# One decode kernel, several edits at once: projection per group, last V load in pieces, V three steps behind K, denominator ahead of the values, K ahead of wq, wq over 128 partitions, wo early in longer rows

## Chip, cores, metric

One core of one Trainium2 chip runs the kernel. The metric is the device time in microseconds (us), median of several executions. Lower is better.

## The reference, cut to what matters

A decode step: one query token, 16 query heads in 8 groups of 2, a cache of 65,536 keys and values per group, head size 256, model width 448. A small mixer runs beside it and is mixed in by a gate.

```python
# cut: setup, mixer, gate
q = (x @ wq).reshape(B, Sq, Hq, Dh)                    # wq: 448 x 4096
scores = einsum("bhqd,bhkd->bhqk", q, k) * Dh ** -0.5  # k, v: 8 groups x 65536 x 256, bf16
p = softmax(scores, axis=-1)
o = einsum("bhqk,bhkd->bhqd", p, v)
a = o.reshape(B, Sq, Hq * Dh) @ wo                     # wo: 4096 x 448
return g * a + (1 - g) * b                             # b: the mixer's row
```

K and V are 537 MB together; with wq and wo 544 MB must come in, once.

## The kernel before

A *chunk* is 2048 keys, a *load* is two chunks of K or of V (2.1 MB). There are 256 chunks, so 128 K loads and 128 V loads, in two K buffers and three V buffers. The SP engine issues loads in pairs, K(n) and V(n-1). A K issue waits until the transposes of the load that held its buffer are done. In each step, PE (TensorE, the matmul engine) transposes chunk s (32 matmuls), computes the scores of chunk s-1 (32), and the values and the denominator of chunk s-2 (32 and 1); this distance of two steps is the *V lag*. VectorE and ScalarE copy the transposed K out of PSUM, the memory that matmuls write to, and ScalarE takes the exponential.

```python
            eng.dma_start(wq_sb, A_wq.rearrange("(kt c) n -> c kt n", c=KCP)).then_inc(sem_wq, 16)

            def k_dma(cd):
                c0 = cd * DC
                g, k = divmod(c0, NCPH)
                slot = cd % KB
                if cd >= KB:
                    eng.wait_ge(sem_tr, NB * ((cd - KB) * DC + DC))
                src = A_k_cache[0, g, k * CH:(k + DC) * CH, :].rearrange("(p n) d -> p (n d)", p=P)
            # ... cut ...
            WO_AT = max(0, NCD - 20)
            for cd in range(NCD + 1):
                if cd < NCD:
                    k_dma(cd)
                if cd - 1 >= 0:
                    v_dma(cd - 1)
                if cd == WO_AT:
                    eng.wait_ge(s_pe_pro, 3)
                    eng.dma_start(wo_sb, A_wo.rearrange("(kt p) n -> p kt n", p=P)).then_inc(sem_wo, 16)

            eng.wait_ge(sem_tail_v, 1)
            eng.dma_start(out_row_ap, out_b[:, :]).then_inc(sem_out, 16)
            eng.wait_ge(sem_out, 16)
            # ... cut ...
            for s in range(NC + 2):
                c = s
                if c < NC:
                    cdk, ck = divmod(c, DC)
                    slot = cdk % KB
                    if ck == 0:
            # ... cut ...
                        for dh in range(2):
                            j = 2 * ntl + dh
                            ins = pe.matmul(sps[:, sbk, 2 * nt:2 * nt + 2],
                                            ktT[:, slotT, bnk, j * P:(j + 1) * P],
                                            qT[:, dh, REP * g:REP * g + REP],
                                            start=(dh == 0), stop=(dh == 1))
                    ins.then_inc(sem_qk, 1)
                cp = c - 2
                if 0 <= cp < NC:
                    g, k = divmod(cp, NCPH)
                    pe.wait_ge(sem_exp, cp + 1)
                    cdv, cv = divmod(cp, DC)
                    vslot = cdv % VB
                    if cv == 0:
                        pe.wait_ge(sem_v[vslot], 16 * (cdv // VB + 1))
                    pslot = cp % PTB
                    for nt in range(NT):
                        for dh in range(2):
                            first = (k == 0 and nt == 0 and dh == 0)
                            last = (k == NCPH - 1 and nt == NT - 1 and dh == 1)
                            col = (g * 2 + dh) * REP
                            pe.matmul(po[:, col:col + REP],
                                      vbuf[:, vslot, cv, nt, dh * P:(dh + 1) * P],
                                      pT[:, pslot, 2 * nt:2 * nt + 2],
                                      start=first, stop=last)
                    ins = pe.matmul(den[0:1, g * 2 * NT:(g + 1) * 2 * NT], ones_col[:, 0:1],
                                    pT[:, pslot, 0:2 * NT], start=(k == 0), stop=(k == NCPH - 1))
                    ins.then_inc(sem_pv, 1)
            # ... cut ...
            pe.wait_ge(s_rden, 1)
            pe.matmul(den[:, RC:RC + HQ], ones_row_f[0:1, 0:P], rden[0:1, :], start=True, stop=True
                      ).then_inc(s_tp, 1)
            pe.wait_ge(s_oTn, 1)
            pe.wait_ge(sem_wo, 16)
            nmm = 2 * HQ
            i = 0
            for hq in range(HQ):
                g, hh = divmod(hq, REP)
                for dh in range(2):
                    col = g * 4 + dh * REP + hh
                    kt = 2 * hq + dh
                    i += 1
                    ins = pe.matmul(sps[0:1, 1, 0:DM], oTn[:, col:col + 1], wo_sb[:, kt, :],
                                    start=(i == 1), stop=(i == nmm))
            ins.then_inc(s_tp, 1)
```

Profile lines name source lines: in the kernel before L277 is the transposes, L293 the scores, L312 the values, L316 the denominator, L339 the projection, L188 and L197 the K and V issues.

The softmax here doesn't subtract the row's maximum and nothing guards it: scores larger than these inputs give would overflow.

## Time and profile before

| | before |
|---|---|
| device time, 3 runs | 1346.64 us (1344.35 to 1348.2) |
| span of the profiled execution | 1353.2 us |
| bytes in | 548 MB |
| mean granted TensorE clock | 0.74 |

The device time is about 1.8 us above the span wherever both are known for one execution. So the profiled execution took about 1355 us. It was slower than any timed one.

The page of the kernel before. Rows are 40 slices of 33.8 us; the clock and DMA rows are in tenths; then the DMA queues (packets, MB, share of 16 engines) and three groups (count, busy us, mean ns, idle before).

```profile
span 1353.2 us, 53303 instructions
...
PEclk9677767768677778676787767766867767777777
DMA  9999999999999999999999999999999999999993
GB/s 302 425 423 411 417 419 425 409 422 412 420 416 416 420 405 423 418 420 407 414 399 402 409 404 414 416 382 402 420 422 419 409 423 398 421 417 416 414 417 160
...
q1 hardware_dynamic: 41454, 544.24, 97.3%
q8 instruction: 198, 3.24, 0.9%
...
L277 PE MATMUL kst<-ident,kbuf 128*128 128x128 bf16 x8192 | 726.0, 269 | 26.0 <-issue 13.7
...
L312 PE MATMUL po<-pT,vbuf 128*128 128x2 bf16 x8192 | 251.3, 164 | 92.2 <-DMA vbuf<-in_A_v_cache_dram 57.5
...
L339 PE MATMUL sps<-wqo,oTn 128*1 128x448 bf16 x32 | 8.1, 424 | 0.6 <-DVE oTn L460 0.6
...
```

The stream runs near 420 GB/s in all slices but the first (302) and the last (160). PE is busy 88% of the span at a clock that changes between full and half. The row q8 is the fetching of instructions: 198 transfers of 16 KB.

Three windows of the same execution; the last three columns are granted clock, DMA share and rate.

```profile
...
core 0: us, PE busy (x) PEld busy (x) DVE busy (x) ACT busy (x) POOL busy (x), PEclk, DMA share, GB/s
...
4.00:20.00 16.00, 1.94 (x46) 1.40 (x45) 6.04 (x26) 1.69 (x3) 0.00 (x0) 1.00 1.00 265
20.00:44.00 24.00, 20.74 (x439) 20.55 (x440) 11.04 (x24) 8.80 (x13) 0.00 (x0) 0.81 1.00 422
44.00:1295.00 1251.00, 1119.29 (x23624) 1091.67 (x23622) 373.97 (x613) 519.62 (x744) 0.00 (x0) 0.74 1.00 414
...
```

From 4 to 20 us the DMA engines are busy all the time, yet only 265 GB/s arrive. That is when wq loads. In the middle the average is 414 GB/s.

What PE waited for (us in total, times, longest us). "issue" is time in which the profile shows no wait.

```profile
...
PE po L312 <- DMA vbuf<-in_A_v_cache_dram: 57.5, 56, 2.5
...
PE po L312 <- issue: 31.4, 32, 2.4
...
PE sps L293 <- issue: 21.2, 28, 1.9
...
PE kst L277 <- issue: 13.7, 17, 1.9
PE kst L277 <- DMA kbuf<-in_A_k_cache_dram: 12.1, 7, 9.6
...
```

PE waits for V, seldom for K. The "issue" times of L312, L293 and L277 sum to 66 us. They lie in the midst of groups of 32 equal matmuls, and their place moves on by 8 matmuls every four steps (13, 21, 29 matmuls left at 102, 122 and 142 us). A step has 97 matmuls with a weight load each, 194 instructions, and some waits. If it has 196, four steps are three blocks of 256 instructions and 16 instructions, or 8 matmuls, more. So I take these for stalls at block borders of the instruction stream; the block size is inferred from this shift.

The end of the timeline (start us, us, engine, line, what):

```profile
...
1339.59 0.19 PE L316 MATMUL den<-pT,ones_col 128*1 128x32 bf16 x1
1339.82 0.41 DVE L448 TENSOR_REDUCE densum<-den 1x16 f32<-1x256 f32 x1 [4.71 <-PE den L316]
...
1341.80 8.07 PE L339 MATMUL sps<-wqo,oTn 128*1 128x448 bf16 x32 [0.60 <-DVE oTn L460]
...
1349.91 0.61 DVE L467 CAST arow_b<-sps 1x448 bf16<-1x448 f32 x1 [7.24 <-PE sps L339]
...
1351.65 0.26 SPq L210 DMA_DIRECT2D out_dram<-out_b  x1
```

The last values end near 1339.7 us. The 32 projection matmuls after them take 8.1 us, and the span ends at 1353.2.

### The profile page before, as it was taken

The page shows a single profiled execution, that of the slowest core. Times are in us where ns is not written, and L with a number is a line of the kernel's source. Part 1 is how long each engine was busy: PE and PEld are TensorE (multiplying, and loading weights), DVE is VectorE, ACT ScalarE, POOL GpSimd, SP SyncE. Part 2 cuts the span into 40 slices and gives each one's busy share as a digit, 9 for nine tenths or more (in the row PEclk, how much of TensorE's full clock was granted, in tenths as well). Part 3 has the DMA queues.
Part 4 walks back from the last instruction along what each step waited for, and adds up shares of the span by engine and source line. Part 5 has one row for each costly group of instructions (what it writes and reads, how often), then busy time and mean ns, then how long its engine had stood idle before and what let it go on. Part 6 is the DMA issues. An engine that isn't in the chain of part 4 may idle for free.

```text
span 1353.2 us, 53303 instructions
## 1 busy us (share of the span) xinstructions
PE 1190.9 (88%) x25055; PEld 1156.5 (85%) x25055; DVE 405.9 (30%) x690; ACT 549.1 (41%) x786; POOL 1.2 (0%) x10
## 2 busy tenths in 40 slices
PE   4889898989989898989999888998899896888997
PEld 4889898889888898989888888888898896888886
DVE  3783222222222222222222222222222221222222
ACT  2454344434344344444434434433444442443442
POOL 0000000000000000000000000000000000000000
PEclk9677767768677778676787767766867767777777
DMA  9999999999999999999999999999999999999993
GB/s 302 425 423 411 417 419 425 409 422 412 420 416 416 420 405 423 418 420 407 414 399 402 409 404 414 416 382 402 420 422 419 409 423 398 421 417 416 414 417 160
DMA packets 41672, 547.65 MB, mean 405 GB/s; under 512 B 4136, under 2 KB 8235, under 8 KB 8238
## 3 DMA queue, kind: packets, MB, share of 16 engines
q1 hardware_dynamic: 41454, 544.24, 97.3%
q8 instruction: 198, 3.24, 0.9%
q14 instruction: 20, 0.16, 0.0%
HBM read 544.22 MB, written 0.00 MB: 402 GB/s over the span
## 4 chain that ended last, share of the span: by engine, by line
DMA 50%; PE 44%; issue 4%; SPq 1%; ACT 0%; DVE 0%; DVEq 0%; ACTq 0%
DMA vbuf<-in_A_v_cache_dram 50%; PE kst L277 28%; PE po L312 9%; PE sps L293 5%; PE den L316 1%; SPq L188 1%; PE sps L339 1%; PE po L322 0%; ACT ktT L497 0%; ACT pT L503 0%; SPq L197 0%; PE den L327 0%; DVE arow_b L467 0%; DVE densum L448 0%; DVE out_b L472 0%
## 5 line engine op out<-in xcount | busy, mean ns | idle before, releaser
L497 ACT ACTIVATE ktT<-kst 128x1024 bf16<-128x1024 bf16 x512 | 513.5, 1022 | 763.6 <-PE kst L277 763.6
L277 PE MATMUL kst<-ident,kbuf 128*128 128x128 bf16 x8192 | 726.0, 269 | 26.0 <-issue 13.7
L277 PEld LDWEIGHTS kst<-ident,kbuf 128*128 128x128 bf16 x8192 | 667.8, 125 | 38.5 <-issue 17.8
L433 DVE COPY ktT<-kst 128x1024 bf16<-128x1024 bf16 x512 | 352.9, 691 | 906.1 <-PE kst L277 894.8
L312 PE MATMUL po<-pT,vbuf 128*128 128x2 bf16 x8192 | 251.3, 164 | 92.2 <-DMA vbuf<-in_A_v_cache_dram 57.5
L312 PEld LDWEIGHTS po<-pT,vbuf 128*128 128x128 bf16 x8192 | 232.0, 99 | 98.3 <-issue 63.5
L293 PE MATMUL sps<-qT,ktT 128*128 128x2 bf16 x8192 | 255.6, 165 | 21.4 <-issue 21.2
L293 PEld LDWEIGHTS sps<-qT,ktT 128*128 128x128 bf16 x8192 | 250.6, 100 | 21.6 <-issue 21.4
L503 ACT ACTIVATE pT<-sps 128x32 bf16<-128x32 f32 x255 | 50.0, 196 | 16.0 <-PE sps L293 15.6
L316 PE MATMUL den<-pT,ones_col 128*1 128x32 bf16 x256 | 46.4, 181 | 0.0
L316 PEld LDWEIGHTS den<-pT,ones_col 128*1 128x1 bf16 x256 | 20.3, 79 | 7.5 <-issue 3.0
L254 PEld LDWEIGHTS sps<-xcol,wqo 112*128 112x128 bf16 x128 | 3.5, 104 | 8.2 <-issue 8.2
L254 PE MATMUL sps<-xcol,wqo 112*128 112x1 bf16 x128 | 3.6, 165 | 7.8 <-DMA wqo<-in_A_wq_dram 7.8
L339 PE MATMUL sps<-wqo,oTn 128*1 128x448 bf16 x32 | 8.1, 424 | 0.6 <-DVE oTn L460 0.6
L485 ACT ACTIVATE tring<-zring 128x448 bf16<-128x448 bf16 x14 | 8.1, 578 | 0.2 <-DVE zring L413 0.2
L339 PEld LDWEIGHTS sps<-wqo,oTn 128*1 128x1 bf16 x32 | 3.0, 98 | 5.3 <-issue 2.5
L244 PE MATMUL sps<-h_row,ones_row_b 1*128 1x448 bf16 x1 | 0.6, 551 | 6.5 <-DVE h_row L387 6.5
L405 DVE TENSOR_TENSOR wring<-uring 128x448 bf16<-128x448 bf16 x14 | 5.5, 393 | 1.4 <-issue 0.4
L407 DVE TENSOR_TENSOR zring<-wring,uring 128x448 bf16<-128x448 bf16 x14 | 5.5, 393 | 1.0
L422 DVE TENSOR_TENSOR gu<-wring,tring 128x448 bf16<-128x448 bf16 x14 | 5.5, 392 | 1.0
L411 DVE TENSOR_TENSOR zring<-uring,wring 128x448 bf16<-128x448 bf16 x14 | 5.5, 392 | 1.0
L244 PEld LDWEIGHTS sps<-h_row,ones_row_b 1*128 1x128 bf16 x1 | 0.1, 100 | 6.5 <-DVE h_row L387 6.5
(70 smaller groups left out, 51.0 us busy)
## 6 DMA issues: line engine op xcount, KB each, us to landing
kbuf<-in_A_k_cache_dram SPq DMA_DIRECT2D x128, 2048.0 KB, 10.6
vbuf<-in_A_v_cache_dram SPq DMA_DIRECT2D x128, 2048.0 KB, 15.2
wqo<-in_A_wq_dram SPq DMA_DIRECT2D x1, 3584.0 KB, 17.5
wqo<-in_A_wo_dram SPq DMA_DIRECT2D x1, 3584.0 KB, 24.9
xrow_b<-in_A_x_dram SPq DMA_DIRECT2D x1, 0.9 KB
grow_b<-in_gate_w_dram SPq DMA_DIRECT2D x1, 0.9 KB
w1row_b<-in_B_w_dram SPq DMA_DIRECT2D x1, 3.5 KB
b1row_b<-in_B_b_dram SPq DMA_DIRECT2D x1, 3.5 KB
```

Source lines behind the costliest of these rows:

```text
L188: eng.dma_start(kbuf[:, slot, :, :, :].rearrange("p c n d -> p (c n d)"), src).then_inc(sem_k[slot], 16)
L254: ins = pe.matmul(sps[:, 1, j:j + 1], wq_sb[0:KCP, kt, col0:col0 + P], xcol[0:KCP, kt:kt + 1], start=(kt == 0), stop=(kt == KC - 1))
L277: ins = pe.transpose(kst[:, b, j * P:(j + 1) * P], kbuf[:, slot, ck, nt, dh * P:(dh + 1) * P], ident[:, :])
L293: ins = pe.matmul(sps[:, sbk, 2 * nt:2 * nt + 2], ktT[:, slotT, bnk, j * P:(j + 1) * P], qT[:, dh, REP * g:REP * g + REP], start=(dh == 0) ...
L312: pe.matmul(po[:, col:col + REP], vbuf[:, vslot, cv, nt, dh * P:(dh + 1) * P], pT[:, pslot, 2 * nt:2 * nt + 2], start=first, stop=last)
L316: ins = pe.matmul(den[0:1, g * 2 * NT:(g + 1) * 2 * NT], ones_col[:, 0:1], pT[:, pslot, 0:2 * NT], start=(k == 0), stop=(k == NCPH - 1))
L339: ins = pe.matmul(sps[0:1, 1, 0:DM], oTn[:, col:col + 1], wo_sb[:, kt, :], start=(i == 1), stop=(i == nmm))
L405: vec.tensor_tensor(W, U, U, op=ALU.mult)
L433: vec.tensor_copy(ktT[:, slotT, b, :], kst[:, b, :]).then_inc(sem_evd, 1)
L485: act.activation(tring[:, slot, :], zring[:, slot, :], AF.Tanh).then_inc(s_tanh, 1)
L497: act.activation(ktT[:, slotT, b, :], kst[:, b, :], AF.Copy).then_inc(sem_eva, 1)
L503: act.activation(pT[:, ce % PTB, :], sps[:, ce % 2, 0:2 * NT], AF.Exp, scale=scale).then_inc(sem_exp, 1)
```

## The change

Its intent: bring the stream up sooner (K first, wq over all partitions, small rows on another queue), let V come later than needed so that PE need not wait for it, and leave little work behind the last load (projection and softmax division per group, the last V in four pieces). The denominator's matmul moves ahead of the values and now has 128 columns of ones. To read wo in long rows, value weights take every second column of V.

```diff
             def v_dma(cd):
                 # ... cut ...
+                for j in range(NPIECE):
+                    eng.dma_start(vbuf[:, slot, j * PN:(j + 1) * PN, :].rearrange("p n d -> p (n d)"),
+                                  cache_src(A_v_cache, cd, j * PN, (j + 1) * PN)).then_inc(sem_vp[j], 16)
-            eng.dma_start(wq_sb, A_wq.rearrange("(kt c) n -> c kt n", c=KCP)).then_inc(sem_wq, 16)
+            k_dma(0)
+            eng.dma_start(wq_a[:, :, :].rearrange("p j n -> p (j n)"),
+                          A_wq[0:WF * P, :].rearrange("(p j) n -> p (j n)", p=P)).then_inc(sem_wq, 16)
+            eng.dma_start(wq_b[:, :], A_wq[WF * P:DM, :].rearrange("r (a n) -> (r a) n", a=2)
+                          ).then_inc(sem_wq, 16)
-            WO_AT = max(0, NCD - 20)
-            for cd in range(NCD + 1):
+            for cd in range(1, NCD + 1):
                 if cd < NCD:
                     k_dma(cd)
-                if cd == WO_AT:
-                    eng.wait_ge(s_pe_pro, 3)
-                    eng.dma_start(wo_sb, A_wo.rearrange("(kt p) n -> p kt n", p=P)).then_inc(sem_wo, 16)
+                v_dma(cd - 1)
+                if cd == KB + 1:
+                    eng.dma_start(wo_sb[:, :, :, :].rearrange("p h j n -> p h (j n)"),
+                                  A_wo.rearrange("(h p j) n -> p h (j n)", h=HQ, j=2)).then_inc(sem_wo, 16)
             # ... cut: PE ...
+            for s in range(NC + LAG):        # LAG = 3
+                if s < NC:
+                    transposes(s)
                 # ... cut: queries at s == 1 ...
+                if 0 <= s - 1 < NC:
+                    scores(s - 1)
+                if 0 <= s - 2 < NC:
+                    denominators(s - 2)
+                if 0 <= s - LAG < NC:
+                    values(s - LAG)
                 # ... cut: mixer ...
+                g, r = divmod(s - LAG - 2, NCPH)
+                if r == NCPH - 1 and 0 <= g < H - 1:
+                    project(g)               # 4 matmuls of group g
+            project(H - 1)
             # ... cut: VectorE; per group: reduce, reciprocal, product, then
+                vec.scalar_tensor_tensor(dst[:, :], acc[0:1, g % 2, PRC:PRC + DM], stat[:, 4:5], run[:, :],
+                                         op0=ALU.mult, op1=ALU.add).then_inc(s_run, 1)
```

## The prediction

> **What bounds the kernel.** The page puts the DMA queue at 97.3% of 16 engines' span; 548 MB cross. Windows of 44 to 1318 us show DMA share 1.00 but 414 GB/s on average, while away from K issues the rate is about 424 GB/s (the Trainium skill, "HBM Reference", Specifications, gives about 425 for a core alone; the trace agrees). The middle is stream-bound with small holes: after K issues that follow the previous one by under 9 us (30 of them) the rate stays 415 to 424; after those that come 10.8 us or later (43) it falls to 340-385 for three microseconds. The holes sum to about 30 us of stream time. A K issue waits for transposes, so PE is co-critical: a step takes 3.6 us at full clock, 5.2 at half (transposes 1.9 or 3.5, scores 0.95, values 0.95), the mean granted clock is 0.74, and two steps must fit in 9.9 us of stream. In late pairs PE lost 0.5 us to V loads and 0.9 to "issue" (the waits: V 57.5 us, 56 times).
>
> **Edges.** Start: from 4 to 20 us, while wq (112 partitions) loads, the windows show 230-350 GB/s; 14.5 MB are in by 44 us, which take 34.5 us at 424. Tail: the stream falls off at 1332 us, values end at 1339.7, the span at 1353.2; 8.1 us of this are 32 projection matmuls.
>
> **The change, costed.**
> 1. K first, wq over 128 partitions, small rows from the other queue: full rate from about 2.5 us. Gain 7 us, all on the stream. K2 is issued near 15 us, when 10 MB queued last to 26, so nothing runs dry.
> 2. Projection and softmax division per group: the last group has 4 matmuls (1.5 us with latency), reduce, reciprocal and product (0.9), one combined row operation (0.75), the store (1.6): 5 us instead of 13.5. Gain 8.5 us. The other groups' matmuls add 7 us of PE, mostly hidden.
> 3. Last V in four pieces, V lag 3: PE no longer idles 2.3 us at 1328 for V; gain 1.5 us.
> 4. V lag 3 in the middle: V waits shrink from 57 us to under 10. PE then waits for K, and K issues come 0.6 us (half clock) to 3 us (full clock) earlier relative to landings. It cannot cure pairs late through half clock or issue stalls. I expect 13 of the 30 us of holes back.
> 5. wo early in rows of 1792 B instead of 896 B: 1 us.
> 6. Cost: ones over 128 columns for denominators, about nothing. V weights are read at stride 2. The skill ("TensorE: Matmul & The Clock Gate", Weight-path perf modes) says fast weight load takes "packed or strided" columns; the trace has only packed ones (0.87 to 0.94 us for 32). I expect no change.
>
> Sum: 7 + 8.5 + 1.5 + 13 + 1 = 31 us, so 1346.6 - 31 = 1316 us. Range 1299 to 1334. Chances: faster 0.57, same 0.38, slower 0.05.
>
> **Signs.** First slice near 395 GB/s instead of 302; under 12 us from the stream's end to the span's; V waits nearly gone, K waits in their place; middle near 419 GB/s with fewer dips after K issues; 32 value weight loads still 0.9 us.
>
> **What would make it wrong.** If strided weight loads are slower, every step grows, and as PE has no room the time rises by 0.3 us x 256 or more. If holes come only from half clock and issue stalls, lag 3 gives nothing: 1329 us. If slack cures all, 1299. If wq is slow for another reason than its layout, 5 us less at the start.

## The result

| | before | after |
|---|---|---|
| device time, 4 runs each | 1345.49 us | 1321.42 us |
| range | 1342.89 to 1348.2 | 1320.36 to 1322.4 |
| ratio | | 0.9827, interval 0.9807 to 0.9848 |

The gain is 24.1 us. It lies within 2% ("same"), while I had given 0.57 to "faster by over 2%". The time lies inside the predicted range, 5 us above the point.

The page of the kernel after:

```profile
span 1320.5 us, 53238 instructions
...
PEclk8787767888777788877778877677878677887776
DMA  9999999999999999999999999999999999999996
GB/s 396 421 425 425 423 417 403 426 425 426 412 409 424 425 416 424 416 411 419 421 420 425 422 414 415 413 414 425 425 416 411 423 419 421 425 416 416 415 419 270
...
q1 hardware_dynamic: 39650, 544.23, 98.4%
q8 instruction: 197, 3.23, 1.0%
...
L245 PE MATMUL kst<-ident,kbuf 128*128 128x128 bf16 x8192 | 695.9, 263 | 143.1 <-DMA kbuf<-in_A_k_cache_dram 137.3
...
L287 PE MATMUL acc<-pT,vbuf 128*128 128x2 bf16 x8192 | 246.0, 163 | 20.1 <-issue 20.0
...
L300 PE MATMUL acc<-wo_sb,oTn 128*1 128x448 bf16 x32 | 10.6, 463 | 2.0 <-issue 1.2
...
```

The first slice rose from 302 to 396 GB/s, the last from 160 to 270. The value matmuls are as quick as before (163 ns against 164), although their weights are read at stride two; in the traces their weight loads take 98 ns against 99.

The windows of the kernel after:

```profile
...
core 0: us, PE busy (x) PEld busy (x) DVE busy (x) ACT busy (x) POOL busy (x), PEclk, DMA share, GB/s
...
4.00:20.00 16.00, 6.43 (x112) 6.25 (x113) 6.43 (x24) 4.58 (x6) 0.00 (x0) 1.00 1.02 435
20.00:44.00 24.00, 19.06 (x493) 18.43 (x489) 13.29 (x33) 10.55 (x17) 0.00 (x0) 0.86 1.00 424
44.00:1295.00 1251.00, 1073.45 (x23997) 1051.01 (x23998) 385.74 (x644) 522.38 (x752) 0.00 (x0) 0.78 1.00 419
...
```

Its waits:

```profile
...
PE kst L245 <- DMA kbuf<-in_A_k_cache_dram: 137.3, 99, 7.5
...
PE acc L287 <- issue: 20.0, 20, 2.1
...
PE sps L261 <- issue: 15.5, 17, 2.3
...
PE kst L245 <- issue: 5.1, 6, 1.5
...
```

The V waits are gone, and PE waits for K instead (137 us). Its end:

```profile
...
1313.95 1.83 PE L287 MATMUL acc<-pT,vbuf 128*128 128x2 bf16 x64
1315.82 0.19 DVE L450 TENSOR_REDUCE densum<-acc 128x2 f32<-128x32 f32 x1 [5.12 <-PE acc L287]
...
1316.54 1.65 PE L300 MATMUL acc<-wo_sb,oTn 128*1 128x448 bf16 x4 [0.76 <-DVE oTn L447]
...
1318.30 0.67 DVE L461 SCALAR_TENSOR_TENSOR out_b<-acc,stat,run 1x448 bf16<-1x448 f32 x1 [1.81 <-PE acc L300]
1319.00 0.32 SPq L216 DMA_DIRECT2D out_dram<-out_b  x1
```

From the last values to the end of the span there are now 4.7 us instead of 13.5.

To compare whole executions, I cut each into three and took off what the bytes would need at 424 GB/s: *start* until 20 MB are in, *middle* from 20 to 532 MB, *tail* from there to the end of the span (from the rates of half-microsecond windows). The three losses and 1291.6 us (547.65 MB at 424 GB/s) sum to the span. *Pace* is the time per 2.1 MB load, between the landings of the 20th and the 200th load, by the later eight of the 16 landings that each load leaves (why the later eight, comes below).

```
kernel               time, median  start  middle  tail   pace
before               1346          9.6    30.3    21.6   5.110   (the slow profiled execution)
before again         1343.8        10.2   18.2    21.9   5.045
after                1321.4        2.6    13.9    12.4   5.040
```

The start gained 7.0 to 7.6 us and the tail 9.2 to 9.5. The middle gained 16 us against the first profile but only 4 against the second. The next section takes these apart.

### The profile page after: what moved, and what is told of

Read it like the earlier page. It is cut to its first block, busy times and chain, and to the rows that moved or that the text cites. A ratio compares the mean times of both kernels' runs of the same rounds, so it can differ in the third digit from the quotient of the medians. Undisturbed runs are those within 1.5% of the kernel's fastest.

```text
span 1320.5 us, 53238 instructions
## 1 busy us (share of the span) xinstructions
PE 1119.0 (85%) x25054; PEld 1094.1 (83%) x25054; DVE 412.6 (31%) x716; ACT 545.7 (41%) x786; POOL 0.9 (0%) x7
## 3 DMA queue, kind: packets, MB, share of 16 engines
q8 instruction: 197, 3.23, 1.0%
## 4 chain that ended last, share of the span: by engine, by line
DMA 56%; PE 42%; issue 1%; DVE 0%; ACT 0%; ACTq 0%; DVEq 0%
DMA kbuf<-in_A_k_cache_dram 56%; PE kst L245 30%; PE acc L287 5%; PE sps L261 5%; DMA b_b<-in_B_b_dram 1%; PE acc L300 1%; PE acc L272 0%; PE sps L339 0%; PE acc L308 0%; ACT L511 0%; PE sps L341 0%; DVE out_b L461 0%; DVE ktT L470 0%; DVE stat L390 0%; ACTq L503 0%
## 5 line engine op out<-in xcount | busy, mean ns | idle before, releaser
L245 PE MATMUL kst<-ident,kbuf 128*128 128x128 bf16 x8192 | 695.9, 263 | 143.1 <-DMA kbuf<-in_A_k_cache_dram 137.3
L245 PEld LDWEIGHTS kst<-ident,kbuf 128*128 128x128 bf16 x8192 | 645.0, 121 | 159.9 <-DMA kbuf<-in_A_k_cache_dram 147.0
L261 PE MATMUL sps<-qT,ktT 128*128 128x2 bf16 x8192 | 251.1, 164 | 15.5 <-issue 15.5
L287 PE MATMUL acc<-pT,vbuf 128*128 128x2 bf16 x8192 | 246.0, 163 | 20.1 <-issue 20.0
L261 PEld LDWEIGHTS sps<-qT,ktT 128*128 128x128 bf16 x8192 | 245.2, 99 | 17.1 <-issue 16.7
L287 PEld LDWEIGHTS acc<-pT,vbuf 128*128 128x128 bf16 x8192 | 227.7, 98 | 26.6 <-issue 26.5
L272 PE MATMUL acc<-pT,ones_sq 128*128 128x32 bf16 x256 | 45.7, 178 | 4.5 <-ACT pT L524 4.1
L272 PEld LDWEIGHTS acc<-pT,ones_sq 128*128 128x128 bf16 x256 | 25.0, 98 | 0.0
L300 PE MATMUL acc<-wo_sb,oTn 128*1 128x448 bf16 x32 | 10.6, 463 | 2.0 <-issue 1.2
L308 PE MATMUL acc<-gu,w2p_b 128*1 128x448 bf16 x14 | 5.1, 363 | 0.0
L420 DVE TENSOR_SCALAR uring<-wring,params 128x448 bf16<-128x448 bf16 x14 | 4.7, 336 | 1.1
## 6 DMA issues: line engine op xcount, KB each, us to landing
vbuf<-in_A_v_cache_dram SPq DMA_DIRECT2D x4, 512.0 KB, 13.5
```

What stands on the lines that cost most here:

```text
L245: ins = pe.transpose(kst[:, b, j * P:(j + 1) * P], kbuf[:, slot, ck * NT + 4 * b + ntl, dh * P:(dh + 1) * P], ident[:, :])
L261: ins = pe.matmul(sps[:, c % 2, 2 * nt:2 * nt + 2], ktT[:, slot, b, j * P:(j + 1) * P], qT[:, dh, REP * g:REP * g + REP], start=(dh == 0), ...
L272: pe.matmul(acc[:, g % 2, DENC:DENC + 2 * NT], ones_sq[:, :], pT[:, c % PTB, :], start=(k == 0), stop=(k == NCPH - 1))
L287: ins = pe.matmul(acc[:, g % 2, col:col + REP], vbuf[:, slot, n, dj:DH:2], pT[:, c % PTB, 2 * nt:2 * nt + 2], start=False, stop=(k == NCPH ...
L300: ins = pe.matmul(acc[0:1, g % 2, PRC:PRC + DM], oTn[:, g % 2, dj * REP + hh:dj * REP + hh + 1], wo_sb[:, g * REP + hh, dj, :], start=(hh ...
```

## The experiments

The theory at first was the prediction's. The stream has holes, stretches in which less than 424 GB/s arrive, because K issues wait for transposes, and these come late when PE waits for V. The rival: the middle gains through something else in the change, or by chance.

### V lag set back to two

```diff
-    LAG = 3
+    LAG = 2
```

> The changed kernel with the V lag set back from three steps to two, all else kept. Theory (the lag lets PE run ahead, so K issues come earlier and the stream has fewer holes): about 1333 us, 1329 to 1338, ratio to the kernel before 0.991; V waits of 40 to 60 us return, the rate in the middle falls from 419 to 414 GB/s, holes from 17 to about 30 us. Rival (the middle gained through fewer instruction stalls, a higher clock or the early wo, not through the lag): 1321 us within 3, ratio 0.982, V waits return but the middle keeps 419 GB/s.

Measured: 1322.18 us, ratio 0.9827. That is the time of the changed kernel (0.9827). The V waits came back, and nothing was lost. Waits of this run:

```profile
...
PE acc L287 <- DMA vbuf<-in_A_v_cache_dram: 106.9, 102, 2.4
...
PE kst L245 <- DMA kbuf<-in_A_k_cache_dram: 21.1, 23, 6.7
...
```

The middle kept 419 GB/s. The theory that the lag made the middle's gain fell here, as far as the changed kernel goes.

### V lag three alone, in the kernel before

```diff
-    PTB = 3
+    PTB = 5
-            for s in range(NC + 2):
+            for s in range(NC + 3):
-                cp = c - 2
+                cp = c - 3
```

> The kernel before with V lag three alone. Theory: 1332 us, 1328 to 1337, ratio 0.990: V waits gone, K waits in their place, middle near 419 GB/s, and 1 to 2 us at the end. Rival: 1345 us within 3, ratio 1.000.

Measured: 1339.12 us, ratio 0.9953 (0.9931 to 0.9975). So the lag does gain 6 to 7 us in the kernel before. That is half of what I expected, and not nothing as the rival had it. Its losses were 9.5, 15.5 and 21.9 us, against 10.2, 18.2 and 21.9 in the second profile of the kernel before: what the two traces show of the gain is nearly all in the middle, and none in the tail.

### All projection at the end

One accumulation of 32 matmuls behind the last group, and one combined row operation, in the changed kernel:

```diff
-                g, r = divmod(s - LAG - 2, NCPH)
-                if r == NCPH - 1 and 0 <= g < H - 1:
-                    project(g)
-            project(H - 1)
+            project_all()
```

> The changed kernel with all 32 projection matmuls at the end, in one accumulation, and one combined row operation; softmax division still per group. Theory: 28 more matmuls at 0.25 us after the last value, all on the chain: plus 6 to 8 us, 1328 us, ratio 0.987. Rival (the projections inside the stream cost PE time that makes K issues late, so the end's gain is partly paid there): plus 0 to 4 us, ratio 0.982 to 0.985.

Measured: 1327.15 us, ratio 0.9863: plus 5.7 us, just under what the theory gave. The trace shows the projection at 7.5 us instead of 1.65. So the end's gain is real, and the projections inside the stream cost nothing that shows.

### wq over 128 partitions alone, in the kernel before

The same bytes with another layout, wrong result:

```diff
-            eng.dma_start(wq_sb, A_wq.rearrange("(kt c) n -> c kt n", c=KCP)).then_inc(sem_wq, 16)
+            eng.dma_start(wqo[:, 0:DM * HQ * DH // P], A_wq.rearrange("r n -> (r n)").rearrange("(p m) -> p m", p=P)).then_inc(sem_wq, 16)
```

(GpSimd also clears the columns that are now not loaded, so that no matmul reads unset memory. The check does not see these faults, so it says little of any variant's arithmetic.)

> The kernel before with only wq's load changed: the same bytes over 128 partitions instead of 112, one run of 28 KB each. Its result is wrong on purpose, as the matmuls still read the old layout. Theory (the layout over 112 partitions makes wq slow): windows of 4 to 20 us near 420 GB/s instead of 240, minus 6 us, 1339.5 us, ratio 0.9955. Rival (the start is slow because the stream is cold or the small rows come first, and K first is what helped): windows stay near 240 GB/s, ratio 1.000.

Measured: 1339.85 us, ratio 0.996 (0.9939 to 0.998), minus 6 us. The window of 4 to 20 us:

```profile
...
4.00:20.00 16.00, 6.41 (x184) 5.85 (x184) 6.30 (x27) 1.69 (x3) 0.00 (x0) 1.00 0.93 396
...
```

It went from 265 to 396 GB/s. The start loss fell to 4.0 us, against 2.6 with K first as well. The layout is most of the start's gain. The layout changes two things, the partitions and the length of the rows (8 KB against 28), and no run parts them. The trace after speaks against the length alone: there the last part of wq, in rows of 4 KB over 128 partitions, took 159 ns a packet, 26 GB/s for one engine, while the 8 KB rows over 112 took 529 ns (median), 15 GB/s.

### The kernel before, again

No edit.

> The kernel before again, for a second profile. The first profile has a span of 1353 us, while its timed runs lie between 1341 and 1350 with a median of 1346, so I expect it to have been a slow execution: a span near 1343 to 1346, the same loss at the start (9.6 us) and in the tail (21.6 us), and a loss in the middle of 20 to 23 us against 424 GB/s instead of 30. If it repeats 30 us, the first profile was typical and the loss in the middle of the wq variant (22 us) needs another cause.

Measured: one run of 1343.83 us, span 1342.0, losses 10.2, 18.2, 21.9. So the first profile was a slow execution, and 9 to 12 us of its 30 us in the middle are not typical. Over all jobs, executions of the kernel before lie between 1341.2 and 1352.6 us, the four of the kernel after, from one job, between 1320.4 and 1322.4. The second is far tighter; this looks like a kernel that stands at a floor.

### wo early, in the kernel before

```diff
-            WO_AT = max(0, NCD - 20)
+            WO_AT = 3
```

> The kernel before with only wo's load moved from the 108th pair of loads to the third; its rows stay 896 B. Lag three gained 6 us in the kernel before, but taking it from the changed kernel cost nothing, so something else there cures the holes. If it is the early wo: minus 4 to 6 us, ratio 0.996. If only the 896 B rows matter and not the place (they cost 2.4 us wherever they are): within 1.5 us, ratio 1.000.

Measured: 1345.97 us, ratio 1.0002 (0.9984 to 1.0021). The place of wo does not matter. The rows may: in the trace before, wo's 896 B rows came in at 338 GB/s for 10 us, in the trace after its 1792 B rows at 399 GB/s for 10 us. At 424 GB/s this is a loss of 2.0 and 0.6 us, so 1.4 us gained by this reading; no run isolates it.

### The denominator ahead of the values, in the kernel before

```diff
+                    pe.matmul(den[0:1, g * 2 * NT:(g + 1) * 2 * NT], ones_col[:, 0:1],
+                              pT[:, pslot, 0:2 * NT], start=(k == 0), stop=(k == NCPH - 1))
                     # ... the 32 value matmuls, the last of which now signals ...
-                    ins = pe.matmul(den[0:1, g * 2 * NT:(g + 1) * 2 * NT], ones_col[:, 0:1],
-                                    pT[:, pslot, 0:2 * NT], start=(k == 0), stop=(k == NCPH - 1))
```

> The kernel before with only the denominator's matmul ahead of the value matmuls of its step instead of behind them, as the changed kernel has it, lag two kept. If the order within the step shifts where PE's instruction stalls fall (69 us in the kernel before, 23 in the changed kernel at lag two) and so cures holes: minus 4 to 6 us, ratio 0.996, stalls under 40 us. If not: within 1.5 us, ratio 1.000, stalls 60 to 70 us.

Measured: 1340.31 us, ratio 0.996 (0.9942 to 0.9978), minus 6 us. One matmul at another place gains as much as the lag. Waits of this run:

```profile
...
PE po L314 <- DMA vbuf<-in_A_v_cache_dram: 93.6, 83, 3.2
...
PE kst L277 <- DMA kbuf<-in_A_k_cache_dram: 20.2, 24, 9.3
...
PE sps L293 <- issue: 8.6, 14, 1.5
...
```

PE's stalls inside groups fell from 66 to 20 us, and its V waits rose from 57 to 94. It spends the same time idle, but at a point where it waits for data. This is the signature of the changed kernel at lag two. The gain itself rests on the timings: the profiled execution was the slowest of its six (1342.24 us), and its losses (9.8, 17.7, 21.3) are hardly below those of the repeated kernel before, which was a quick one. Why this order keeps the stalls away is open.

So two parts of the change, each alone, gain 6 us by the timings; that the order's gain lies in the middle is inferred, as it touches nothing at the ends. In the changed kernel the order does without the lag; the lag without the order was not run there. Both seem to run into the same floor. What is it?

### Three K buffers

In the changed kernel; wo is loaded over wq's memory to make room.

```diff
-    KB = 2
+    KB = 3
-        wq_a = sb([P, WF, NQ], bf16, "wq_a")       # and wq_b, wo_sb
+        wqo = sb([P, HQ * 2 * DM], bf16, "wqo")    # wq_a, wq_b and wo_sb are views of it
                 if cd == KB + 1:
+                    eng.wait_ge(s_q, 1)
```

> The changed kernel with three K buffers instead of two; to make room, wo is loaded over wq once the queries are done. Theory (what is left of the holes, 14 us, comes from K issues that wait for transposes): K issues one to two steps earlier, the middle at 422 to 424 GB/s, holes under 5 us: 1311 us, 1307 to 1315, ratio 0.975. Rival (the stream itself dips, or PE's tempo bounds the middle): 1321 us within 3, ratio 0.982, dips after K issues as before.

Measured: 1321.65 us, ratio 0.9817 (0.9796 to 0.9839): no gain. Yet the dips behind the K issues did go. The rate of the core in the microseconds after a K issue, for issues that came late, and for comparison early:

```
                         K issues   rate in GB/s, 0-1, 1-2, 2-3, 3-4, 4-5 us after the issue
before, interval < 9 us        30   423  422  422  415  423
before, 10.8 to 11.5 us        27   412  346  365  385  414
after,  < 9 us                 29   423  422  429  425  425
after,  10.8 to 11.5 us        12   412  402  343  418  406
three K buffers, 10.8 to 11.5  15   418  421  430  427  409
```

A hole that can be removed without any gain was not lost time. The landing records of the trace show why. Each load leaves 16 landings there, and 16 data packets are in flight at a time, so I read a landing as the end of one DMA engine's share. With three K buffers, the 16 landings of one load, against the last of them (mean of loads 80 to 239, us):

```
three K buffers   -12.6 -12.6 -12.5 -12.4 -12.3 -12.1 -11.7 -11.1   -1.9 -1.6 -1.4 -1.2 -1.0 -0.7 -0.5 0.0
after              -4.6  -4.6  -4.5  -4.4  -4.2  -4.1  -3.7  -3.1   -2.0 -1.5 -1.2 -1.0 -0.8 -0.5 -0.2 0.0
```

Eight engines run ahead as far as the buffers let them, and eight are behind. Between loads 20 and 60, while the first eight were still free to run, they took 4.902 us per load and the others 5.036. The slow eight never lacked work: between loads 20 and 239, the next load had been issued at least 11.8 us before the first of them landed the current one, while for the first of the fast eight it was at times only 0.7 us. So the slow eight set the time; when the core's rate dips, it is the fast eight that have nothing left. That is also why the middle lost less here (10.7 us) and the tail more (15.5): the fast eight end 12 us before the slow ones.

Now the pace column can be read. The slow eight take 5.036 to 5.040 us per load in the kernel after, at lag two, with the projection at the end, with one last piece, with three K buffers and with both. The kernel before had 5.110 in its first profile, and 5.045, 5.062 and 5.066 in three executions with its middle unchanged (the repeat, the wq variant, the wo variant). V lag three in it gave 5.038, and the denominator first 5.049, in the slowest of its six executions. By 256 loads, an excess of 0.007 to 0.028 us is 2 to 7 us. That is all that the middle had to give, except in a slow execution.

### Fewer instructions

Why are eight engines slow? They might carry PE's instruction fetches as well: 197 transfers that take 1.05 us each in the trace are 206 us of engine time, by eight engines and 256 loads 0.10 us per load. The difference to be explained is 0.134. To test this, most value matmuls were left out, then also most score matmuls, both wrong, with three K buffers (and the last V load in two pieces instead of four):

```diff
-                for nt in range(NT):      # values
+                for nt in range(1):
-                for nt in range(NT):      # scores, second run only: 32 matmuls become one
+                ins = pe.matmul(sps[:, c % 2, 0:2 * NT], ktT[:, slot, 0, 0:P],
+                                qT[:, :, :].rearrange("p a b -> p (a b)"), start=True, stop=True)
```

> Three K buffers, and of the 32 value matmuls of a chunk only two are left, so the result is wrong on purpose. With three K buffers the landings of one load by its 16 engines split into two groups of eight, 12 us apart; where the queue never ran dry the slow eight took 5.04 us per load of 2 MB and the fast eight 4.90. Theory (the slow eight also carry the fetches of PE's instructions, 197 of 16 KB at 1.04 us each): without 15,000 of 50,000 instructions about 137 fetches are left, the difference falls from 0.134 to about 0.09 us per load, the slow pace to 5.00, and the time by some 10 us for that and up to 4 us in the tail for the missing work: about 1309 us. Rival (these eight are slower by themselves, through their place or port): the slow pace stays within 0.01 of 5.04 and the time falls only by the tail's 4 us, 1318 us.

> As the run with few value matmuls, and of the 32 score matmuls of a chunk one is left, over all query columns; wrong on purpose. Theory: about 75 fetches, the difference between slow and fast engines about 0.05 us per load, slow pace near 4.95, about 1297 us. Rival: slow pace 5.04, 1316 us.

Measured: 1307.88 us (ratio 0.9712) and 1295.61 us (0.9622), each within 2 us of the theory and far from the rival. The row of instruction fetches on the pages of the three kernels, first with all matmuls:

```profile
...
q8 instruction: 197, 3.23, 1.0%
...
```

with few values:

```profile
...
q8 instruction: 137, 2.24, 0.7%
...
```

with few values and few scores:

```profile
...
q8 instruction: 75, 1.23, 0.4%
...
```

```
fetches   slow eight   fast eight   difference   (us per load, loads 20 to 60)
197       5.036        4.902        0.134
137       4.988        4.904        0.084
 75       4.940        4.907        0.033
```

The pace of the fast eight does not move, and that of the slow eight falls with the fetches. The first step made 13.8 us for 60 fetches, the second 12.3 for 62. By the pace of the slow eight from load 20 to 200 (5.038, 4.994 and 4.947 us, times 256), 11 and 12 us are theirs. Part of it falls in the tail, whose loss went from 15.5 to 13.4 and 11.9 us (against the bytes of each run), as the last steps had less work and the engines were less far apart. In the last run the middle came in at 427 GB/s (44 to 1265 us), so 424 is a yardstick here and no ceiling.

That PE had less to do can't be the cause of the pace. It already waited 130 us for K with all its matmuls, and in the three runs the next load had been issued at least 11.8, 12.5 and 13.6 us before the slow eight needed it.

The trace does not name the engine of a packet, but it shows whom the fetches delay. In the run with 75 fetches, take the steps from one load's landings to the next, loads 20 to 236. In 154 of them no fetch starts, in 62 one does. The slow eight took 4.907 us without a fetch and 5.043 with one, the fast eight 4.903 in both cases. (The difference of 0.14 becomes 0.10 or 0.17 if all fetches are set half a microsecond earlier or later; that of the fast eight stays under 0.01.) And half a microsecond into a fetch 15.0 data packets are in flight on average, a microsecond before it 16.0. So the fetches delay these eight engines alone, and without a fetch these are as fast as the others. At 0.14 us, 197 fetches are 0.10 us per load, as estimated; whether the rest of the 0.134 is theirs too stays open.

### Three K buffers and lag two

> Three K buffers with the V lag set to two. With three K buffers the middle lost 10.7 us against 424 GB/s instead of 13.9, but the tail 3 us more, as the last V load had to wait for a V buffer while the stream ran dry. At lag two V buffers come free a step earlier: the tail as in the changed kernel or 1 us better, the middle as with three K buffers: 1317.5 us, 1315 to 1321, ratio 0.979. If the tail does not come back: 1321.

Measured: 1320.22 us, ratio 0.9807 (0.9782 to 0.9832). The tail did not come back (15.5 us), for the reason above: what counts is when the slow eight end. No version with the right result is clearly faster here than the kernel after.

### The last V load whole

```diff
-    PN = 8
+    PN = 32
```

> The changed kernel with the last V load whole instead of in four pieces. The trace after shows PE reaching the last chunk pair's values at 1313.9 us without waiting, while the pieces landed by about 1311 us; so I expect no change: 1321 us within 2, ratio 0.982. If the pieces matter as intended: plus 2 to 4 us.

Measured: 1321.14 us, ratio 0.981 (0.9785 to 0.9836), no change. PE came to the last values late anyway: in the tail it had two chunks of transposes at half clock before it.

## Why the prediction was right or wrong, point by point

1. **Start, 7 us.** Right. The start loss went from 9.6 or 10.2 us to 2.6, and the layout of wq alone made 6 us. One detail was wrong: "K2 is issued near 15 us". It was issued at 20.05, as the small rows landed only at 13.1 us behind K and wq, and PE stood still until then. The queued 10 MB covered it.
2. **Projection and division per group, 8.5 us.** Right: 13.5 became 4.7 us behind the last values, and 5.7 of these 8.8 us came back when only the projection was undone.
3. **Last V in pieces and lag at the end, 1.5 us.** Wrong, nothing: whole or in pieces is the same time, and lag three alone left the tail at 21.9 us. PE's own steps last longest there, not the wait for V.
4. **Middle, "13 of the 30 us of holes back".** This is the mis-sized term. It measured 6 us by the timings of the two parts that each reach the floor. Two steps failed. First, I read the holes on one profiled execution of 1353.2 us and took the gain off a timed median of 1346.6; the repeat lost 18.2 us there, not 30.3. Second, "stream-bound with small holes" took a dip of the core's rate below 424 GB/s for lost time. The three-buffer run showed dips removed without gain: the time is that of the eight slower engines, which the instruction fetches delay, 5.04 us per load. The rate in the middle did become the predicted 419 GB/s, but that hit is mostly luck: the repeat of the kernel before had 418, not 414.
5. **V lag as the cause.** Half right. V waits went to zero and K waits came, as said. But lag three is one of two parts that do the same, and without it the changed kernel is as fast. The matmul order I did not price at all.
6. **wo, 1 us.** About 1.4 us by the trace, not isolated. The early place is worth nothing.
7. **Strided weights and wide ones, no cost.** Right, 163 ns per value matmul against 164, and 98 ns per weight load against 99. What the Trainium skill's page "TensorE: Matmul & The Clock Gate", Weight-path perf modes, says of strided columns agrees.

With the measured sizes the sum is 7 + 8.8 + 0 + 6 + 1.4 = 23 us; 24.1 were measured. The sizes come from different executions and from timings and traces alike, so that they meet within 1 us is in part luck.

## What to carry to other kernels

Compare the profiled execution's span with the timed runs before reading losses off it, and do not add a gain read on a slow execution to a median. When a stream is near its ceiling, look at the landings of the single DMA engines and not only at the core's rate: here a dip cost no time while the slowest engines had work. And count the instruction fetches: here they came through the same DMA engines as the data, and 60 fetches fewer were worth 12 to 14 us, a third K buffer nothing. This was shown on kernels with a wrong result; none with the right result and fewer instructions was run.

## What the Trainium skill lacked or had wrong

- "Runtime: NRT & Kernel Launch", Instruction fetch mechanics, has the fetch in blocks of 16 KiB through a DMA queue of its own. The trace agrees: 197 transfers, 3.23 MB. It calls the cost "mostly hidden". Here it is not: PE stalled 20 to 66 us, by kernel, in the midst of matmul groups, which I take for block borders, and some 60 fetches fewer made 12 to 14 us, tail included.
- No page says that a core's 16 DMA engines can split into eight fast and eight slow on equal shares. Here it is 4.902 against 5.036 us per load of 2.1 MB, and 12.6 us on average between the first and the last landing of one load. Nor does one say that PE's instruction fetches delay eight of the 16 alone: 5.043 us for a load with a fetch against 4.907 without, and 4.903 for the other eight.
- "HBM Reference", Specifications, gives about 425 GB/s for a core alone. The core's rate reaches that in single windows; over the middle of the best kernels here it is 419 to 421, as the slower engines set the pace, and with 75 fetches instead of 197 it is 427.
- "DMA: Bandwidth & Descriptors", Rules for kernel authors, advises 128 partitions, without a figure for less. Here a load over 112 partitions in rows of 8 KB came at 265 GB/s and the same bytes over 128 in rows of 28 KB at 396, beside the first K and V loads, in the window of 4 to 20 us.
